# Rounding two weight blocks in turns, and the last block product of one group placed behind the first of the next

## The chip, the core and the metric

The kernel runs on one core of one Trainium2 chip. The metric is the time on the device in microseconds (us). The kernel before takes 807.48 us, the median of three runs that lie between 807.12 and 807.95 us. The execution that was profiled spans 805.8 us.

## The reference

The computation is a linear attention with a normalised output, followed by an MLP-Mixer block that mixes first over tokens and then over channels. All tensors are float32 outside; the four MLP weights come as float64.

```python
# q, k, v: 8 batches x 8 heads x 576 tokens x 64
kv  = einsum('bhsd,bhse->bhde', k, v)
o   = einsum('bhsd,bhde->bhse', q, kv)
o   = o / sqrt(mean(o * o, axis=-1) + 1e-06) * g_norm
x   = o.transpose(0, 2, 1, 3).reshape(8, 576, 512)
# token mixing: w_tok1 576 x 256, w_tok2 256 x 576
h   = maximum(x^T @ w_tok1, 0) @ w_tok2
u   = x + h^T
# channel mixing: w_ch1 512 x 1536, w_ch2 1536 x 512
out = u + maximum(u @ w_ch1, 0) @ w_ch2
```

## The kernel before

The kernel has three stages. In the first (to about 200 us) it loads queries, keys and values, runs attention for pairs of batches and token mixing for the pair before, and in between makes float32 weights out of the raw float64 words ("rounding"). In the second (200 to 273 us) it runs the channel mixing of a first group of tokens with a fast matrix product of seven block products in place of eight. In the third it runs the eight other groups with two levels of that scheme.

**Rounding.** A block of weights goes through one fetch (a DMA by the Sync engine's queue), one scaling on ScalarE, and six steps on VectorE. Each of the last five needs the one before; `power` begins a second tile, `part`. There are four buffers for raw blocks, and one for `part`.

```python
def decode(dst, raw):
    def scale():  nc.scalar.activation(dst, hi word of raw, AF.Copy, scale=2.0 ** -112)
    def clamp():  nc.vector.tensor_scalar(out=dst, in0=dst, ... min, max)
    def shift():  nc.vector.tensor_scalar(out=bits, in0=bits, 3, logical_shift_left)
    def sign():   nc.vector.scalar_tensor_tensor(out=bits, in0=hi word of raw, ..., in1=bits)
    def power():  nc.vector.tensor_scalar(out=part, in0=bits, 0xFF800000, bitwise_and)
    def lower():  nc.vector.scalar_tensor_tensor(out=part, in0=low word of raw, ..., in1=part)
    def both():   tensor_add(dst, dst, part)
    return scale, clamp, shift, sign, power, lower, both

def block(n, loads, dst):           # (fetch, scale, clamp, shift, sign, power, lower, both)
    def fetch():
        raw.append(stage.tile([P, n, 2], U32, name="raw", tag="raw", bufs=4))
        for o, i in loads(raw[0]):
            dma(o, i)
    ...
    return (fetch,) + decode(dst, turn)
```

Five token blocks (`w0` to `w4` in the lists below, the digit behind being the step) and fourteen channel blocks are rounded. The channel blocks run as one stream of 85 steps. A number in a list takes so many steps from it. `stream` of before rounds one block after the other; the scaling of the next block goes with `lower`, and the fetch of the block four further on with `both`:

```python
def stream(blocks, ahead=4):
    steps = [blocks[0][1]]
    for n, block in enumerate(blocks):
        steps += block[2:]
        for at, m, k in ((-2, n + 1, 1), (-1, n + ahead, 0)):
            if m < len(blocks):
                steps[at] = do(lambda *fs: [f() for f in fs], steps[at], blocks[m][k])
    return iter(steps)
```

**The order of the first stage.** Every engine takes its instructions in the order of these lists. `kv` and `a` are attention's products on TensorE, `e` their copies (ScalarE), `g` the gain (VectorE), `q` squares (ScalarE), `t` sums of squares, `m r i` mean, root and inverse, `s` eight scalings of a row (ScalarE), `l` and `lq` loads. `h` and `hr` are the first token product (`hr` ends with four ReLUs on ScalarE), `u` the second, and `z` the seed of a `u`, a copy by ScalarE into the PSUM bank (`ps_u`) to which the product then adds.

```python
def steady(n0, n1):
    return [
        "kv00 l00 e00 1 -s40", "h00 3", "kv01 l01 e01 1", "h01 3", f"a0 q00 g01 q01 g00 {n0}",
        "h10 1 t00 t01 2", "h11 4", "hr 2 z2", "a1 q10 g11 q11 g10 1", "kv10 l10 e10 t10 t11 m0 r0 1",
        "u0 i0 1", "kv11 l11 e11", "u1 1 s00", "u2 z4 1", "a2 q20 g21 q21 g20", "u3 s01 t20 t21",
        "u4 z6 1", "a4 q40 g41 q41 g40 lq0", "u5 s10 t40 t41 1", "a3 q30 g31 q31 g30 lq1",
        "u6 s11 t30 t31 m2 r2 1 i2 p20 p21 s30", f"u7 1 s31 {n1}", "u8 2"]
...
# start, middle (12 steps of the stream), steady(3, 1), steady(0, 0), last
```

**The first group's second product.** Seven block products, each of 24 matmuls, into four PSUM tiles; three of the tiles are used twice.

```python
def channel2_once(g):
    ...
    p1, p6, p7, p5 = (m_psum(shape, f"ps_w{n}") for n in (1, 6, 7, 5))
    ...
    def fourth():
        product(4, p7, False, True)
        tensor_add(quarter(1, 0), p7, quarter(1, 0))
        store(g, xg, 1)
    def third():
        product(3, p5, False, True)
        tensor_add(quarter(0, 1), p5, quarter(0, 1))
        store(g, xg, 0)
    return [first, sixth, second, seventh, fifth, fourth, third]
```

**The other groups.** PSUM has a pool `m` of six banks and a pool `c` of two. In each of the inner products the first small product goes into bank `a`; ScalarE (or VectorE) copies what is there into bank `c`, and TensorE then adds the second product to that copy, with `start=False`. The products are numbered places; what else is to be done goes `beside` a place.

```python
PLACE = {1: 0, 2: 8, 6: 3, 5: 4, 7: 6, 4: 9, 3: 12}      # the next inner product begins at 7
    def read_first():
        banks["c"] = late["c"].tile([P, DM], F32, name="ps_c")[:, :size]
        read(fit(banks["c"]), 0, 0)
    at(1, "a", True, False, read_first)
    at(6, "a", False, False, lambda: read(temp("u2", 2), 0, 1))
    ...
    at(2, "c", False, True, lambda: take(0, 0, "c", act))
```

**The seam between the two.** `weave` spreads sums of weights and their stores (32 of them) between the steps of the first group. Then come two "marking products": one matmul of 384 columns each into the two `c` banks, whose result nobody reads, so that TensorE has written the banks before copies are put there and added to.

```python
body = [step for pair in zip(channel2_once_steps, extra) for step in pair]
weave(body, lasts + [f for fs, _ in inner2 for f in fs] + [f for _, f in inner1])
fetch_x(1, 0)
fetch_x(1, 1)
for place in range(2):
    t = late["c"].tile([P, DM], F32, name="ps_c")
    step = do(matmul, t[:, :FQ], lhsT=w_ch1[:, 0, 0, :P], rhs=w_ch1[:, 0, 0], start=True, stop=True)
    put(place, step) if place else step()
```

Of the kernel before, what the change touches and what calls it, by code (L numbers as in the profile page):

```python
# [11 lines left out]
F32 = mybir.dt.float32  # L12
# [7 lines left out]
def kernel(  # L20
# [33 lines left out]
    P = 128  # L54
    B, S, DM = k.shape
# [11 lines left out]
    FQ = FH // 2  # L67
# [31 lines left out]
    w_ch1 = consts.tile([P, 4, 4, FQ], F32, name="w_ch1")  # L99
# [6 lines left out]
    def do(f, *a, **kw):  # L106
        return lambda: f(*a, **kw)

    late = {}
# [4 lines left out]
    def dma(o, i, engine=nc.sync):  # L114
        keep(engine.dma_start(o, i))  # L115

    def tensor_add(o, a, b, op=ALU.add, engine=nc.vector):
        keep(engine.tensor_tensor(out=o, in0=a, in1=b, op=op))  # L118
# [4 lines left out]
    def copy(o, a):  # L123
        keep(nc.scalar.copy(o, a))  # L124

    def matmul(*a, **kw):
        keep(nc.tensor.matmul(*a, **kw))  # L127
# [170 lines left out]
    def w2_of(n):  # L298
        i = {1: 0, 7: 1, 2: 2, 3: 3}
        return w_ch2[:, i[n]] if n in i else late["d2"][:, {5: 0, 6: 1, 4: 2}[n]]  # L300
# [263 lines left out]
    def fetch_x(g, i):  # L564

        if g < NG:
            if i == 0:
                xg[g] = late["xg"].tile([P, J, DM], F32, name="xg")
            dma(xg[g][:, ts(i, 2)], u_dram[g].rearrange("(t p) e -> p t e", p=P)[:, ts(i, 2)])
# [11 lines left out]
    blocks, blocks_dram = {}, {}  # L581
# [37 lines left out]
    def m_psum(shape, name):  # L619
        return late["m"].tile(shape, F32, name=name, tag="m")  # L620
# [17 lines left out]
    def r_tile():  # L638
        return late["r"].tile([P, 2, DH], F32, name="r", tag="r")
# [63 lines left out]
    def channel2_once(g):  # L703

        shape = [P, 2, DH]
        x = xg[g]
        quarter = lambda i, j: x[:, 2 * i:2 * i + 2, ts(j, DH)]

        def product(n, ps, start, stop):
            for p in range(2):  # L710
                for s in range(NS):
                    matmul(ps[:, p], lhsT=late["once"][n - 1][:, s, p], rhs=w2_of(n)[:, s],
                           start=(start and p == 0 and s == 0), stop=stop,
                           skip_group_check=True)

        p1, p6, p7, p5 = (m_psum(shape, f"ps_w{n}") for n in (1, 6, 7, 5))
        t1, u2, u3 = (r_tile() for _ in range(3))

        def first():
            product(1, p1, True, False)  # L720
            copy(t1, p1)

        def sixth():
            product(6, p6, True, True)
            tensor_add(u2, p6, t1)

        def seventh():
            product(7, p7, True, False)
            tensor_add(u3, p7, u2)
            tensor_add(quarter(0, 1), quarter(0, 1), u2)  # L730
            tensor_add(quarter(1, 0), quarter(1, 0), u2)

        def fifth():
            product(5, p5, True, False)
            tensor_add(u3, p5, u3)
            tensor_add(quarter(1, 1), quarter(1, 1), u3)

        def second():
            product(2, p1, False, True)
            tensor_add(quarter(0, 0), p1, quarter(0, 0))  # L740
# [12 lines that stand above are left out]
# [7 lines left out]
    def put(place, *steps):  # L760
        beside[place] += steps

    def outer(place, size, mul, to, base=None, act=copy, onto=False):

        banks, t = {}, {}

        def product(n, name, start, stop):
            if start:
                banks[name] = m_psum([P, size], f"ps_{name}")
            mul(n, banks[name], start, stop)

        def temp(n, bufs):
            t[n] = late["tmp"].tile([P, FQ], F32, name=n, tag=n, bufs=bufs)[:, :size]
            t[n] = fit(t[n])
            return t[n]

        def fit(flat):
            return flat if size == P else flat.rearrange("p (w t) -> p w t", w=W)

        def read(o, i, j):

            if base:
                tensor_add(o, fit(banks["a"]), base(i, j))
            else:
                copy(o, fit(banks["a"]))

        def read_first():
            banks["c"] = late["c"].tile([P, DM], F32, name="ps_c")[:, :size]
            read(fit(banks["c"]), 0, 0)

        def write(i, j, name, n):
            tensor_add(to(i, j), fit(banks[name]), to(i, j) if onto else t[n])

        def put_on(i, j, n):
            if onto:
                tensor_add(to(i, j), to(i, j), t[n])  # L800

        def take(i, j, name, act):
            if onto:
                tensor_add(to(i, j), banks[name], to(i, j))
            else:
                act(to(i, j), fit(banks[name]))

        def at(n, name, start, stop, *steps):
            def all_of():
                product(n, name, start, stop)  # L810
                for step in steps:
                    step()

            products[place + PLACE[n]] = all_of

        at(1, "a", True, False, read_first)
        at(6, "a", False, False, lambda: read(temp("u2", 2), 0, 1))
        at(5, "b", True, False)
        at(7, "a", False, False, lambda: read(temp("u3", 1), 1, 1))
        at(2, "c", False, True, lambda: take(0, 0, "c", act))  # L820
        put(place + PLACE[7] + (1 if onto else 2), do(put_on, 1, 1, "u3"), do(write, 1, 1, "b", "u3"))
        at(4, "a", False, True, lambda: take(1, 0, "a", copy) if onto else read(to(1, 0), 1, 0))
        put(place + PLACE[4], do(put_on, 0, 1, "u2"))
        at(3, "b", False, True)
        put(place + PLACE[3] + 1, do(write, 0, 1, "b", "u2"))
# [200 lines left out]
    def store(g, x, i):  # L1026
        x = x[g]
        if g < B:
            dma(out[g, ds(2 * i * P, 2 * P)].rearrange("(t p) e -> p t e", p=P),
                              x[:, 2 * i:2 * i + 2])  # L1030
        else:
            store_rest({B: x}, 2 * i)
            store_rest({B: x}, 2 * i + 1)
# [5 lines left out]
    def weave(body, fill):  # L1039
        done = 0  # L1040
        for n, step in enumerate(body):
            step()
            upto = len(fill) * (n + 1) // len(body)
            while done < upto:
                fill[done]()
                done += 1

    def stream(blocks, ahead=4):


        steps = [blocks[0][1]]
        for n, block in enumerate(blocks):
            steps += block[2:]
            for at, m, k in ((-2, n + 1, 1), (-1, n + ahead, 0)):
                if m < len(blocks):
                    steps[at] = do(lambda *fs: [f() for f in fs], steps[at], blocks[m][k])
        return iter(steps)

    def play(lines, after={}, **stages):
# [38 lines left out]
    for block in tok1[2:] + tok2:  # L1098
# [5 lines left out]


    start = [
        "kv00 e00 l00 j14 w01 w11 w02 w03 w04 w05 w06 w07 w12 w13 w14 w15 w16 w17", "kv01 j10 e01 l01 f0",
        "a00 g00 q00", "a01 g01 q01 t00", "a10 g10 q10 t01 m0 r0", "a11 g11 q11 t10 i0 p00 p01",
        "kv10 j6 t11 m1 r1 e10 i1 s10 p11", "kv11 j2 e11", "h000 h001 h002 h003", "a20 g20 q20", "a21 g21 q21 t20",
        "h010 t21 m2 r2", "a30 g30 q30 i2 p20", "a31 g31 q31 t30", "h011 t31 m3 r3 p21", "a40 i3 p30 g40 q40 p31",  # L1110
        "h012 h013 t40 m4 r4 w21 i4 s40 lq0 l10 l11"]
    middle = [
        "kv00 e00 w31 w22 w23 w24", "h10 w25 w26 w27 f1 -lq1 l00 w32 w33 w34", "kv01 e01 l01 w41 w35 w36 w37",
        "h11 f2 w42 w43 w44", "hr w45 w46 w47 f3", "a0 q00 g01 q01 g00 t00 t01", "u0 z2 1", "u1 1",
        "a1 q10 g11 q11 g10 t10 t11 m0 r0", "u2 i0 1", "kv10 e10 z4 s00", "u3 1 s01", "kv11 e11 1",
        "u4 1 z6", "a2 q20 g21 q21 g20 s10", "u5 t20 t21 2", "a4 q40 g41 q41 g40 lq0 l10 l11", "u6 t40 t41 2",
        "a3 q30 g31 q31 g30 lq1 s11", "u7 t30 t31 m2 r2 1 i2 p20 p21 s30", "u8 1 s31"]
# [38 lines left out]
    first = ExitStack()  # L1156
# [47 lines left out]
    n = len(sums1) // 3  # L1204
# [8 lines left out]
             lambda: [f() for f in outer_u(1)], lambda: [f() for f in inner_u(1, 0, 7)]]  # L1213
    extra += [lambda: None] * (len(channel2_once_steps := channel2_once(0)) - len(extra))
    body = [step for pair in zip(channel2_once_steps, extra) for step in pair]
    weave(body, lasts + [f for fs, _ in inner2 for f in fs] + [f for _, f in inner1])
    fetch_x(1, 0)
    fetch_x(1, 1)


    for place in range(2):
        t = late["c"].tile([P, DM], F32, name="ps_c")
        step = do(matmul, t[:, :FQ], lhsT=w_ch1[:, 0, 0, :P], rhs=w_ch1[:, 0, 0], start=True, stop=True)
        put(place, step) if place else step()
    for n, (_, f) in enumerate(inner2):
        put(8 + n, f)
    for g in range(1, NG):
# [42 lines left out]
```

## Time and profile before

| engine | busy us | share of 805.8 us | instructions |
|---|---|---|---|
| TensorE, matmuls | 788.6 | 98% | 7012 |
| TensorE, weight loads | 694.4 | 86% | 7012 |
| VectorE | 683.3 | 85% | 1308 |
| ScalarE | 302.2 | 38% | 838 |
| GpSimd | 79.6 | 10% | 75 |

The page calls the engines PE (matmuls), PEld (weight loads), DVE (VectorE), ACT (ScalarE), POOL (GpSimd) and SP (the Sync engine, whose queue issues the DMAs). A group of instructions is named by its line in the kernel, its engine, and output<-inputs. L163 is the scaling of a raw block, L166 to L187 are the rounding steps, L118 is every addition and subtraction, L121 a ReLU, L124 a copy, L421 the gain, L425 a square, L475 a row scaling, L127 every matmul. `raw<-in_moe_w_ch_dram` is the fetch of a raw channel block, `ps_w` the first group's second product, `ps_a`, `ps_b` and `ps_c` the inner products of the other groups.

Some rows of the groups that the change touches:

| what | count | mean ns of one |
|---|---|---|
| scaling of a channel block, 768 / 1024 columns (ScalarE) | 8 / 6 | 912 / 1160 |
| clamp, 768 / 1024 (VectorE) | 8 / 6 | 550 / 684 |
| shift, 768 / 1024 | 8 / 6 | 548 / 690 |
| sign, 768 / 1024 | 8 / 6 | 956 / 1329 |
| power, 768 / 1024 | 8 / 6 | 638 / 725 |
| lower, 768 / 1024 | 8 / 6 | 1116 / 1224 |
| both, 768 / 1024 | 8 / 6 | 1046 / 1216 |
| `ps_w` matmul, 256 columns (TensorE) | 168 | 379 |

Busy time is an average over stages that have different limits, and a busy TensorE includes matmuls whose ends are modelled. What a step is worth is therefore read from the wait that ends last in its own stretch of time. Idle time of an engine that nobody waits for costs nothing.

### The profile page before, as it was taken

The page shows a single profiled execution, that of the slowest core. Times are in us where ns is not written, and L with a number is a line of the kernel's source. Part 1 is how long each engine was busy: PE and PEld are TensorE (multiplying, and loading weights), DVE is VectorE, ACT ScalarE, POOL GpSimd, SP SyncE. Part 2 cuts the span into 40 slices and gives each one's busy share as a digit, 9 for nine tenths or more (in the row PEclk, how much of TensorE's full clock was granted, in tenths as well). Part 3 has the DMA queues.
Part 4 walks back from the last instruction along what each step waited for, and adds up shares of the span by engine and source line. Part 5 has one row for each costly group of instructions (what it writes and reads, how often), then busy time and mean ns, then how long its engine had stood idle before and what let it go on. Part 6 is the DMA issues. An engine that isn't in the chain of part 4 may idle for free.

```text
span 805.8 us, 17651 instructions
## 1 busy us (share of the span) xinstructions
PE 788.6 (98%) x7012; PEld 694.4 (86%) x7012; DVE 683.3 (85%) x1308; ACT 302.2 (38%) x838; POOL 79.6 (10%) x75
## 2 busy tenths in 40 slices
PE   6999999999999999999999999999999999999997
PEld 6645554544888899999999999999999999999997
DVE  4688989999886978978987997997898899799687
ACT  1357585664110134234234234332424423423331
POOL 1210101010000011012003003001101200300300
PEclk9999999999999999999999999999999999999999
DMA  9999998436458567468467648738836855863642
GB/s 289 320 345 351 334 354 304 158 119 208 150 175 294 194 210 239 131 221 267 149 201 240 201 153 259 234 118 262 265 119 217 262 166 181 250 201 123 218 147 83
DMA packets 97346, 175.51 MB, mean 218 GB/s; under 512 B 7024, under 2 KB 54128, under 8 KB 97264
## 3 DMA queue, kind: packets, MB, share of 16 engines
q1 hardware_dynamic: 95584, 172.65, 66.6%
q10 hardware_dynamic: 1680, 1.74, 0.7%
q8 instruction: 55, 0.90, 0.5%
q14 instruction: 27, 0.22, 0.1%
HBM read 137.79 MB, written 36.57 MB: 216 GB/s over the span
## 4 chain that ended last, share of the span: by engine, by line
PE 83%; DVE 6%; DMA 5%; ACT 3%; SPq 1%; issue 1%; ACTq 0%; DVEq 0%
PE ps_a L127 37%; PE ps_b L127 19%; PE ps_c L127 9%; PE ps_v L127 5%; PE ps_w L127 4%; PE ps_u L127 4%; DMA v_in<-in_v_dram 3%; PE ps_h L127 2%; ACT x L475 1%; SPq L115 1%; DMA raw<-in_moe_w_ch_dram 1%; DMA k_in<-in_k_dram 1%; DVE ms L442 1%; DVE part L187 1%; DVE x L421 1%; PE ps_o L127 1%
## 5 line engine op out<-in xcount | busy, mean ns | idle before, releaser
L124 ACT COPY u<-ps_a 128x128 f32<-128x128 f32 (+1 forms) x160 | 56.1, 351 | 156.6 <-PE ps_a L127 156.6
L118 POOL TENSOR_TENSOR v<-v,v 128x384 f32<-128x384 f32 (+1 forms) x48 | 61.4, 1301 | 532.8 <-ACT v L124 492.8
L127 PE MATMUL ps_b<-uT,sums 128*128 128x128 f32 x672 | 86.2, 276 | 0.0
L127 PEld LDWEIGHTS ps_b<-uT,sums 128*128 128x128 f32 x672 | 80.7, 192 | 0.2
L118 DVE TENSOR_TENSOR v<-v,v 128x768 f32<-128x768 f32 (+1 forms) x86 | 79.5, 932 | 1.1
L127 PE MATMUL ps_a<-uT,w_ch 128*128 128x128 f32 x576 | 78.9, 275 | 0.0
L124 ACT COPY ps_c<-ps_a 128x128 f32<-128x128 f32 (+1 forms) x80 | 26.9, 336 | 129.5 <-PE ps_a L127 129.5
L118 DVE TENSOR_TENSOR v<-ps_b,u 128x384 f32<-128x384 f32 x112 | 61.5, 549 | 12.3 <-PE ps_b L127 10.6
L127 PEld LDWEIGHTS ps_a<-uT,w_ch 128*128 128x128 f32 x576 | 71.4, 192 | 0.4
L127 PE MATMUL ps_u<-h,w_tok 128*128 128x512 f32 (+1 forms) x160 | 68.0, 608 | 1.6 <-ACT h L121 0.6
L127 PE MATMUL ps_h<-x,w_tok 128*128 128x512 f32 (+1 forms) x160 | 65.9, 604 | 0.0
L118 DVE TENSOR_TENSOR uT<-uT 128x512 f32<-128x512 f32 (+4 forms) x103 | 63.1, 629 | 0.8
L127 PE MATMUL ps_a<-uT,w 128*128 128x128 f32 x432 | 60.0, 275 | 0.0
L127 PEld LDWEIGHTS ps_a<-uT,w 128*128 128x128 f32 x432 | 54.0, 192 | 0.0
L127 PEld LDWEIGHTS ps_h<-x,w_tok 128*128 128x128 f32 (+1 forms) x160 | 25.9, 189 | 31.1 <-issue 28.3
L127 PEld LDWEIGHTS ps_u<-h,w_tok 128*128 128x128 f32 (+1 forms) x160 | 24.5, 178 | 31.9 <-issue 24.9
L121 ACT ACTIVATE v<-v 128x384 f32<-128x384 f32 (+1 forms) x86 | 42.5, 528 | 23.0 <-DVE v L118 22.5
L118 DVE TENSOR_TENSOR sv<-v 128x384 f32<-128x384 f32 x80 | 43.4, 551 | 8.9 <-ACT v L121 8.9
L118 DVE TENSOR_TENSOR xg<-xg,r 128x512 f32<-128x512 f32 x74 | 50.0, 686 | 0.7
L475 ACT ACTIVATE x<-x,inv 128x64 f32<-128x64 f32 x184 | 46.0, 336 | 9.6 <-DVE inv L461 9.6
L127 PE MATMUL ps_a<-sums,sv 128*128 128x128 f32 x336 | 47.1, 276 | 0.0
L127 PE MATMUL ps_a<-uT,sums 128*128 128x128 f32 x336 | 46.8, 275 | 0.0
(134 smaller groups left out, 1576.5 us busy)
## 6 DMA issues: line engine op xcount, KB each, us to landing
sums<-sums SPq DMA_DIRECT2D x112, 576.0 KB, 4.4
qT<-in_q_dram SPq DMA_DIRECT2D x8, 1152.0 KB, 9.6
xt<-u_dram SPq DMA_DIRECT2D x36, 256.0 KB, 4.0
blocks<-y SPq DMA_DIRECT2D x72, 128.0 KB, 2.7
uT<-blocks SPq DMA_DIRECT2D x36, 256.0 KB, 4.9
xg<-u_dram SPq DMA_DIRECT2D x18, 512.0 KB, 5.1
k_in<-in_k_dram SPq DMA_DIRECT2D x16, 512.0 KB, 9.2
u_dram<-x SPq DMA_DIRECT2D x16, 512.0 KB, 4.9
```

Of the source, the lines that this page charges most:

```text
L115: keep(engine.dma_start(o, i))
L118: keep(engine.tensor_tensor(out=o, in0=a, in1=b, op=op))
L121: keep(nc.scalar.activation(o, a, AF.Relu))
L124: keep(nc.scalar.copy(o, a))
L127: keep(nc.tensor.matmul(*a, **kw))
L187: keep(nc.vector.scalar_tensor_tensor(out=part[0], in0=raw()[..., 0], scalar=2.0 ** -52, in1=part[0], op0=ALU.mult, op1=ALU.mult))
L421: keep(nc.vector.tensor_mul(x, bank[c, h], g_sb.to_broadcast([P, number(c), D])))
L442: keep(nc.vector.tensor_reduce(stats_of(c)[0][:, h], sq[c, h], axis=AX.X, op=ALU.add))
L475: keep(nc.scalar.activation(x[:, k, h], x[:, k, h], AF.Copy, scale=inv[:, k, h]))
```

## The change

It has four parts. The stream of channel blocks takes the first three steps of one block (clamp, shift, sign) in turns with the last three of the block before (power, lower, both), so that neighbours on VectorE don't need each other; the scaling of the next block now goes with `shift`, and the fetch of a further block with `lower`. The lists of the first stage do the same by hand for the token blocks. The first group's tiles `p7` and `p5` come from the pool `c`, so that their products are TensorE's writes into these two banks, and the marking products go. And the step `third` leaves the woven part, and runs behind the first product of the next group, where TensorE has otherwise to wait for ScalarE's copy.

```diff
-        p1, p6, p7, p5 = (m_psum(shape, f"ps_w{n}") for n in (1, 6, 7, 5))
+        p1, p6 = (m_psum(shape, f"ps_w{n}") for n in (1, 6))
+        p7, p5 = (late["c"].tile(shape, F32, name="ps_c", tag="c") for _ in range(2))
...
-            banks["c"] = late["c"].tile([P, DM], F32, name="ps_c")[:, :size]
+            banks["c"] = late["c"].tile([P, DM], F32, name="ps_c", tag="c")[:, :size]
...
     def stream(blocks, ahead=4):
+        def all_of(*fs):
+            return do(lambda: [f() for f in fs])
         steps = [blocks[0][1]]
-        for n, block in enumerate(blocks):
-            steps += block[2:]
-            for at, m, k in ((-2, n + 1, 1), (-1, n + ahead, 0)):
-                if m < len(blocks):
-                    steps[at] = do(lambda *fs: [f() for f in fs], steps[at], blocks[m][k])
+        second = [None] * 3
+        for n in range(len(blocks) + 1):
+            first = list(blocks[n][2:5]) if n < len(blocks) else [None] * 3
+            if n + 1 < len(blocks):
+                first[1] = all_of(first[1], blocks[n + 1][1])
+            if second[1] and n - 1 + ahead < len(blocks):
+                second[1] = all_of(second[1], blocks[n - 1 + ahead][0])
+            steps += [f for pair in zip(first, second) for f in pair if f]
+            second = list(blocks[n][5:8]) if n < len(blocks) else second
         return iter(steps)
...
     start = [
-        "kv00 e00 l00 j14 w01 w11 w02 w03 w04 w05 w06 w07 w12 w13 w14 w15 w16 w17", ...
+        "kv00 e00 l00 j14 w01 w11 w02 w03 w04 w12 w05 w13 w06 w14 w07 w15 w16 w17", ...
     middle = [
-        "kv00 e00 w31 w22 w23 w24", "h10 w25 w26 w27 f1 -lq1 l00 w32 w33 w34", "kv01 e01 l01 w41 w35 w36 w37",
-        "h11 f2 w42 w43 w44", "hr w45 w46 w47 f3", ...
+        "kv00 e00 w31 w22 w23 w24", "h10 w41 w25 w32 w26 w33 w27 w34 f1 -lq1 l00", "kv01 e01 l01 w35 w42 w36 w43",
+        "h11 w37 w44 f2", "hr w45 w46 w47 f3", ...
...
     body = [step for pair in zip(channel2_once_steps, extra) for step in pair]
+    behind = body.pop(-2)
     weave(body, lasts + [f for fs, _ in inner2 for f in fs] + [f for _, f in inner1])
-    fetch_x(1, 0)
-    fetch_x(1, 1)
-    for place in range(2):
-        t = late["c"].tile([P, DM], F32, name="ps_c")
-        step = do(matmul, t[:, :FQ], lhsT=w_ch1[:, 0, 0, :P], rhs=w_ch1[:, 0, 0], start=True, stop=True)
-        put(place, step) if place else step()
+    put(0, behind, do(fetch_x, 1, 0), do(fetch_x, 1, 1))
```

## The prediction

> **What bounds the kernel now.** I read the page's first three parts, then the chain of waits, then the busy time by stretch, and then the stretches in which TensorE is not full.
>
> ```profile
> PE 788.6 (98%) x7012; PEld 694.4 (86%) x7012; DVE 683.3 (85%) x1308; ACT 302.2 (38%) x838; POOL 79.6 (10%) x75
> ...
> PE 83%; DVE 6%; DMA 5%; ACT 3%; SPq 1%; issue 1%; ACTq 0%; DVEq 0%
> ```
>
> TensorE is busy for 788.6 of 805.8 us and is 83% of the chain. A change that takes time off VectorE can therefore win only where TensorE waits: 17.2 us in all. The busy time by stretch (TensorE first, its weight loads, then VectorE, then ScalarE) says where that is:
>
> ```profile
> 60.00:80.00 20.00, 18.64 (x305) 10.28 (x304) 16.98 (x34) 14.82 (x49) 0.00 (x0) 1.00 1.03 351
> 80.00:100.00 20.00, 20.00 (x220) 10.02 (x216) 19.34 (x28) 9.77 (x31) 2.79 (x2) 1.00 1.08 336
> 100.00:120.00 20.00, 19.16 (x277) 10.48 (x270) 17.49 (x34) 16.26 (x47) 0.00 (x0) 1.00 1.07 350
> 120.00:140.00 20.00, 20.00 (x186) 9.93 (x185) 18.96 (x28) 12.89 (x41) 2.39 (x2) 1.00 0.86 323
> 140.00:160.00 20.00, 19.65 (x275) 10.49 (x274) 19.13 (x30) 12.54 (x33) 0.00 (x0) 1.00 0.40 138
> ```
>
> From 80 to 160 us, where most channel weights are rounded, VectorE is over 87% busy, and yet TensorE idles only 0.84 + 0.35 = 1.2 us there (80.00 less the four sums). The transfers are full to 140 us (shares near 1). So I asked what ScalarE, which opens each block's rounding with a scaling, waits for. The chain of waits between 98 and 124 us (start, length, work):
>
> ```profile
> 90.85 9.13 DMA raw<-in_moe_w_ch_dram
> ...
> 100.00 0.94 ACT w_ch L163
> 100.95 1.95 ACT h L121 x4
> 102.89 0.49 ACT ps_u L124
> 103.38 0.53 ACT sq L425
> ...
> 109.34 1.76 ACT x L475 x7
> 111.11 0.47 ACT x L124
> 111.58 0.48 ACT ps_u L124
> ```
>
> The reader is to see that a raw weight block lands at 99.98, that its scaling starts at 100.00, and that everything ScalarE owes TensorE (four ReLUs, the seed copies into `ps_u`, the squares) follows in file. The table of waits gives this one as 7.7 us. The next block's transfer, asked of the raw tile in the window where it is issued:
>
> ```profile
> L115 SPq DMA_DIRECT2D raw<-in_moe_w_ch_dram x1: 520/520/520, 96.2 to 96.2; - x1
> ...
> DMA to landing us min/median/max: 9.7/9.7/9.7
> ```
>
> It lands at 96.2 + 9.7 = 105.9. I come back to that number.
>
> **What the Trainium skill says.** "VectorE: DVE Perf Modes", section "The DRAIN you can't avoid", says that the next operation doesn't start until the pipe has emptied, so that a chain can't be made cheaper by order. The timeline of VectorE differs: after a clamp of 128x768 that takes 0.55 us, the dependent shift starts 0.58 us on (84.81 to 85.39), but an independent operation only 0.47 us on (72.82 to 73.29). I go by the trace: a dependence costs 0.11 us. "PSUM — Partial Sum Buffer", "The four PSUM rules", says that writes of VectorE and ScalarE neither set nor clear the bits that decide whether a matmul adds or overwrites; only matmuls do. That is what the marking products are for. The trace can show their time, not the bits. "Perfetto Trace Analysis", "Optimization Strategy", says to find the gaps of the busiest engine and what releases it; I follow it above.
>
> **The change part by part.** *Rounding in turns.* The block's six VectorE steps are clamp, shift, sign, power, lower, both; five of them depend on the one before. Fourteen channel blocks make 70 such pairs, of which 42 stand directly together in the timeline now (other work lies between the rest): 42 x 0.11 = 4.6 us of VectorE. As TensorE waits 1.2 us in 80 to 160, nearly all of it is off the path. For the token weights (128x576 steps) I laid the new order out from 47.04, where the first scaling ends: it finishes at 54.5 where it finished at 54.6, because the second block's first clamp must still wait for that scaling and now holds up the block before it. Worth 0.1.
>
> *What moves with it.* Counting the steps of the two orders: the scaling of block m stood at step 6m and stands at 6m - 5; the fetch of block m moves from 6(m - 4) + 7 to 6(m - 4) + 8, which is the same place in the DMA queue. So a block is scaled five steps earlier after an unchanged transfer. By the lines of `steady`, block 5's scaling goes from step 30 to 25, both between the squares at 91 us and the ReLUs: it still waits for 99.98. Block 6's scaling goes from step 36 (behind `kv11`, at 106.81 now) to step 31, in `hr`, directly behind the ReLUs, which end at 102.89. Its data lands at 105.9. ScalarE then stands 3.0 us and scales for 0.9 us, to 106.85, before the seed copy `z2` and the squares, which began at 102.89 and 103.38 before: 4.0 us later.
>
> What of it reaches TensorE: `u2` waits for the seed until 107.35, where it began at about 107.05: 0.3. The gain that follows the first square goes from 103.93 to 107.95, the mean from 106.31 to about 110.0, the inverse's end from 109.06 to 112.7, the eight scalings and the next seed (2.0 + 0.5 + 0.5) to 115.7. `u4` began at 112.11 with this seed, having waited for it, so TensorE is 3.6 us late there. Block 7's scaling (0.9 us) moves from step 42, where nobody waited, to step 37, in `u2`, ahead of the next squares, in a stretch where ScalarE is busy without a break: about 0.9 more. Some 4.7 us in this stretch. In the next pair block 12's scaling (1.06 us) goes behind the seed `z6`, and a `both` (1.22) before the last gains is replaced by a shift (0.69): the 1.12 us that TensorE waits at 160.8 falls by about 0.6.
>
> *The end of the first group.* The chain there:
>
> ```profile
> 236.70 36.26 PE ps_w L127 x168
> 272.96 0.65 PE ps_c L127 x2
> 273.60 0.67 PE ps_a L127 x6
> 274.27 0.65 PE ps_c L127 x2
> 274.92 0.84 PE ps_a L127 x6
> ```
>
> The two `ps_c` rows are the marking products: 1.30 us on TensorE's own path, removed whole. The second one filled the time in which ScalarE copies `ps_a`; the block product of 24 matmuls (168 / 7, 36.26 / 7 = 5.2 us) now fills it, so the 0.84 falls to 0.67 as well: 1.47 us. Against this stands VectorE's backlog: the add that frees the fourth product's bank ran at 271.98, though the product ended at 267.6, and the weaving over 13 places instead of 14 puts one more sum (0.47) in front of it. The copy into that bank then ends near 273.65, just as TensorE comes to need it; the last block product's add comes behind all the sums, near 277.6, and its bank is wanted again at about 277.65: a wait of up to 0.5. Net gain 1.0 to 1.5; I take 1.3.
>
> The sum: 807.5 - 0.1 + 4.7 - 0.6 - 1.3 = 810.2 us.
>
> **Rivals.** *All gain:* block 6's data lands before 103, or ScalarE isn't held by it. Then about -1.3 - 0.6 - 0.6 (part of the waits in 60 to 120) remains: 805.0. For it: transfers of the same size also took 6.2 us (the one issued at 71.4). Against it: the landing is governed by a full queue ahead of it, whose order doesn't change. *VectorE is the real bound:* 4.6 us less work on an engine 97% busy between 80 and 100 would give up to 4 us: 803.5. Against it: TensorE's 20.00 of 20.00 there. *A knock-on:* as clamps wait for the blocked scalings, VectorE stands from about 97.5 to 100.95, and the raw buffers are freed 2 to 3 us later, so that the fetches behind them and the key and value loads in the same queue are late: 813. Against it: those loads are used 15 us later. *A worse end:* the new wait for banks after the first group is 2 us, not 0.5: 812.
>
> **Range and chances.** I give the mechanism of block 6 about 70%, with 809 to 812 behind it, the all-gain case 20% near 805, the rest to worse. Predicted 810.2, range 805.0 to 813.0. Both ends are within 1% of the time before; 2% is 16 us, nearly all the idle time TensorE has. Faster by over 2%: 0.01; within 2%: 0.97; slower by over 2%: 0.02.
>
> **What would show it.** Right: in the changed kernel's waits a second wait of ScalarE for a raw channel block, near 103 and about 3 us long; TensorE waiting for `ps_u` copies near 107 and 112; no `ps_c<-w_ch` rows near 273; dependent rounding steps replaced by pairs 0.08 us inside each other. Wrong: ScalarE's only wait for raw weights still the one before 100 us, and less TensorE idle time between 100 and 125. It would also be wrong if the group boundary showed TensorE idle by over 1 us.

## The result, and the profile after

The changed kernel takes 813.56 us, the median of four runs (812.25 to 813.89), beside 807.3 us for the kernel before in the same comparison: a ratio of 1.0074, 95% interval 1.0057 to 1.0091. It is 6.3 us slower, where 2.9 had been predicted. The execution that was profiled is the fastest of the four (812.25 us); it spans 810.5 us, 4.7 more than before.

The page after, engines' busy time and the chain that ended last:

```profile
PE 786.6 (97%) x7008; PEld 692.1 (85%) x7008; DVE 678.9 (84%) x1308; ACT 301.2 (37%) x838; POOL 79.2 (10%) x75
...
PE 81%; DVE 8%; DMA 5%; ACT 4%; issue 1%; SPq 1%; ACTq 0%; DVEq 0%
```

VectorE has 4.4 us less to do and TensorE 2.0 (the marking products among it), and yet the span is longer: TensorE's idle time grew from 17.2 to 23.9 us. The busy time by stretch says where (the columns are TensorE, its weight loads, VectorE, ScalarE):

```profile
60.00:80.00 20.00, 18.17 (x294) 9.88 (x294) 16.10 (x32) 15.32 (x50) 0.00 (x0) 1.00 0.91 311
80.00:100.00 20.00, 20.00 (x218) 10.07 (x216) 17.56 (x27) 9.19 (x31) 2.39 (x2) 1.00 1.08 347
100.00:120.00 20.00, 15.16 (x225) 8.22 (x218) 12.55 (x24) 11.77 (x31) 0.00 (x0) 1.00 0.99 314
120.00:140.00 20.00, 19.14 (x245) 9.84 (x244) 19.50 (x33) 16.13 (x55) 2.39 (x2) 1.00 0.89 310
140.00:160.00 20.00, 20.00 (x250) 10.72 (x247) 18.09 (x29) 8.81 (x19) 0.00 (x0) 1.00 0.46 165
```

Between 100 and 120 us TensorE, VectorE and ScalarE all do less than before (19.16, 17.49 and 16.26 then). Three engines that are idle at once wait for a fourth thing. The chain of waits through that stretch (start, length, work) names it:

```profile
97.17 9.34 DMA raw<-in_moe_w_ch_dram
106.50 0.02 issue
106.53 0.91 ACT w_ch L163
107.43 0.48 ACT ps_u L124
107.91 0.53 ACT sq L425
...
109.08 0.95 DVE w_ch L174
...
113.64 0.36 DVE inv L461
...
116.52 0.07 ACT ps_u L124
```

Block 6's transfer lands at 106.50; its scaling is in front of the seed copy and the squares, and these in front of mean, root, inverse and the next seed. On TensorE (the last column is the idle time before, and what ended it):

```profile
102.74 1.99 PE L127 MATMUL ps_u<-h,w_tok 128*128 128x512 f32 x4 [1.02 <-ACT h L121]
...
111.90 0.93 PE L127 MATMUL ps_o<-kvp,qT 64*64 64x64 f32 x48 [1.56 <-ACT kvp L124]
...
117.05 1.98 PE L127 MATMUL ps_u<-h,w_tok 128*128 128x512 f32 x4 [2.12 <-ACT ps_u L124]
...
122.55 1.16 PE L127 MATMUL ps_o<-kvp,qT 64*64 64x64 f32 x64 [0.86 <-ACT sq L425]
```

These are 5.6 us of waits; in the kernel before, only the first and the third exist:

```profile
101.97 1.98 PE L127 MATMUL ps_u<-h,w_tok 128*128 128x512 f32 x4 [0.57 <-ACT h L121]
...
112.11 1.98 PE L127 MATMUL ps_u<-h,w_tok 128*128 128x512 f32 x4 [0.21 <-ACT ps_u L124]
```

The place of TensorE's instructions against the kernel before sums the whole up: +0.3 us when the first pair of batches is done (79 us), +5.7 at 129 us and still +5.7 when the first stage ends (205.85 against 200.17), +4.7 at the first `ps_b` behind the seam (280.30 against 275.59), +4.7 at the end.

The end of the first group, in the chain of waits:

```profile
278.32 0.61 DVE xg L118
...
279.02 0.47 ACT ps_c L124
...
279.53 0.49 PE ps_a L127 x2
```

No marking product is left, and the last block product lies behind the first product of the next group. From the first `ps_w` to the first `ps_b` it is 38.09 us instead of 39.06: 0.97 less.

### The profile page after: what moved, and what is told of

Same layout as the page of the kernel before. It is cut to its first block, busy times and chain, and to the rows that moved or that the text cites. A ratio compares the mean times of both kernels' runs of the same rounds, so it can differ in the third digit from the quotient of the medians.

```text
span 810.5 us, 17648 instructions
## 1 busy us (share of the span) xinstructions
PE 786.6 (97%) x7008; PEld 692.1 (85%) x7008; DVE 678.9 (84%) x1308; ACT 301.2 (37%) x838; POOL 79.2 (10%) x75
## 3 DMA queue, kind: packets, MB, share of 16 engines
q10 hardware_dynamic: 1680, 1.74, 0.7%
## 4 chain that ended last, share of the span: by engine, by line
PE 81%; DVE 8%; DMA 5%; ACT 4%; issue 1%; SPq 1%; ACTq 0%; DVEq 0%
PE ps_a L127 37%; PE ps_b L127 19%; PE ps_c L127 10%; PE ps_v L127 4%; PE ps_h L127 4%; PE ps_u L127 4%; PE ps_w L127 2%; ACT x L475 2%; DVE ms L442 1%; DMA k_in<-in_k_dram 1%; DMA raw<-in_moe_w_tok_dram 1%; DMA v_in<-in_v_dram 1%; DMA raw<-in_moe_w_ch_dram 1%; DVE x L421 1%; PE ps_o L127 1%
```

## The experiments

The theory: a scaling that stands in ScalarE's file ahead of its data holds everything behind it, and that is the loss; the turns themselves and the seam cost nothing. The rivals: the turns (VectorE's order) are the loss; the seam is; late key and value loads are.

### The parts alone: seam, turns, and the scaling's place

`seam_only` is the changed kernel with the stream and the lists of before. `turns_only` is the kernel before with the new stream of channel blocks and nothing else. `scale_early` is the kernel before, in which VectorE still rounds one block after the other, and only the scaling goes five steps ahead:

```diff
-        steps = [blocks[0][1]]
+        steps = [do(lambda *fs: [f() for f in fs], blocks[0][1], blocks[1][1])]
...
-            for at, m, k in ((-2, n + 1, 1), (-1, n + ahead, 0)):
+            for at, m, k in ((-1, n + 2, 1), (-1, n + ahead, 0)):
```

`turns_late_scale` is the changed kernel, turns and seam and all, with the scaling of the next block three steps later:

```diff
-            if n + 1 < len(blocks):
-                first[1] = all_of(first[1], blocks[n + 1][1])
...
+            if n + 1 < len(blocks):
+                at = second if n else first
+                at[2] = all_of(at[2], blocks[n + 1][1])
```

> The kernel before with the change at the seam alone: tiles p7 and p5 from the pool c, no marking products, the last block product behind the next group's first; lists and stream of rounding steps as before. If the loss of 6.3 us comes from the rounding stream (my theory), this runs about 1.0 us faster than before (1.30 us of marking products less about 0.3 us of new waits), 806.3, and TensorE starts the first group's product at the same time as before (ps_v near 200). If the seam itself costs time (rival: new waits for the two banks), it is slower than before.

> The kernel before with the new stream of rounding steps alone (two blocks in turns, scaling five steps earlier); token lists and seam as before. Theory: it carries the whole loss and lacks the gain of the seam, so 6 to 7.5 us slower than before, with two waits of ScalarE for raw channel blocks, the second of about 3 us near 103 us. Rival (the loss comes from the token lists or the seam): within 1 us of before.

> The kernel before with one thing moved: the scaling of block m goes with the last step of block m - 2 (step 6m - 5, as in the changed kernel) and VectorE's order stays one block after the other. Theory (ScalarE held by the transfer of block 6): the loss comes from the place of the scaling, so 4.5 to 7.5 us slower than before, with the second wait of ScalarE near 103 us. Rival (the order on VectorE, which puts longer steps before gains and sums, costs the time): within 1 us of before.

> The changed kernel with one thing moved: the scaling of the next block goes with the step both, three steps later, just before its own clamp (step 6m - 2). Block 6 is then scaled behind the roots in kv10, after about 106.5 us, when its data has landed. Theory: the second wait of ScalarE goes, and the kernel takes 805.5 to 807, about 1 us less than before (the seam), as the saved dependences on VectorE lie off TensorE's path. Rival 1 (order on VectorE costs the time): stays above 811. Rival 2 (VectorE is the bound once ScalarE is free): below 804.

| run | median us (runs) | before | ratio, 95% interval | first stage ends |
|---|---|---|---|---|
| seam_only | 807.02 (13) | 807.35 | 0.9993, 0.9985 to 1.0002 | 199.91 |
| turns_only | 813.88 (5) | 807.35 | 1.0077, 1.0063 to 1.0090 | 206.09 |
| scale_early | 813.51 (5) | 807.35 | 1.0067, 1.0055 to 1.0080 | 207.00 |
| turns_late_scale | 807.02 (21) | 807.35 | 0.9996, 0.9989 to 1.0002 | 199.33 |

("First stage ends" is the start of the first `ps_v` in the profiled execution; 200.17 for the kernel before.)

The loss follows the scaling's place, and nearly all of it is there without the new order of VectorE. With the old order and an early scaling it is there; with the new order and a later scaling it is gone. ScalarE's timeline in `scale_early` has the second wait for a raw block, with VectorE's order untouched:

```profile
100.44 2.05 ACT L121 ACTIVATE h<-ps_h 128x512 f32<-128x512 f32 x4
105.47 0.90 ACT L163 ACTIVATE w_ch<-raw 128x768 f32<-128x768 f32 x1 [2.98 <-DMA raw<-in_moe_w_ch_dram]
106.27 0.57 ACT L124 COPY ps_u<-x 128x512 f32<-128x512 f32 x1
```

and that of `turns_late_scale` has it no longer: the seed copy follows the ReLUs directly, and the scaling comes after its data, which landed at 107.17.

```profile
101.70 2.06 ACT L121 ACTIVATE h<-ps_h 128x512 f32<-128x512 f32 x4
103.60 0.64 ACT L124 COPY ps_u<-x 128x512 f32<-128x512 f32 x1
...
107.93 0.91 ACT L163 ACTIVATE w_ch<-raw 128x768 f32<-128x768 f32 x1
```

`scale_early` doesn't lose its time in quite the same places, though. At 129 us it is 4.7 us behind the kernel before, and the changed kernel 5.7: about 1 us, or somewhat more, comes with the turns. After that, `scale_early` loses some time to the clock. Behind a wait of 1.74 us, TensorE's granted clock is at half for 3.4 us (the third number from the end), and 16 matmuls of a second token product take 7.26 us, 1.7 more than the 5.57 in the changed kernel:

```profile
168.20:171.60 3.40, 3.40 (x7) 1.44 (x5) 3.37 (x8) 1.61 (x5) 0.00 (x0) 0.50 0.89 295
```

The same is seen once more there, from 117.0 to 120.4, and nowhere in the two profiles of the changed kernel but in the last 3 us. The only one of the five runs of `scale_early` with a mean clock of 1.0 took 812.19 us, 4.8 more than before. So the scaling's place alone is worth some 4.7 us, and not the full 6.2 of the medians.

So "the turns are the loss" and "the seam is the loss" fall. `turns_late_scale` came out at the upper edge of its expectation (807.02, of 805.5 to 807); `seam_only` fell short of its own (807.02, not 806.3). The seam alone changes the time by something between -1.2 and +0.2 us, by its interval.

### The same file, an earlier transfer

If the wait is for the transfer, then the changed kernel must recover without any change to ScalarE's order, when the raw block lands earlier. In the one queue, four key and value loads stand directly in front of the fetch of block 6, and four others in front of that of block 5. `fetch_first` moves the first four behind the fetch, `fetch_both` all eight. `after_again` is the changed kernel once more.

```diff
 fetch_first
-            ... "kv01 l01 e01 1", "h01 3", f"a0 ...
+            ... "kv01 e01 1", "h01 3 l01", f"a0 ...
 fetch_both, in addition
-            "kv00 l00 e00 1 -s40", "h00 3", ...
+            "kv00 e00 1 -s40", "h00 3 l00", ...
```

> The changed kernel with one thing moved: in the steady list the load l01 of keys and values stands behind the three steps after it, so that the fetch of block 6 is issued before it, some 5 us earlier (near 92 us instead of 97.2), and should land near 102 instead of 106.5. VectorE's and ScalarE's orders stay as changed. Theory (what costs is that ScalarE reaches block 6's scaling before its transfer has landed): the second wait of ScalarE (2.9 us) goes, and 3.5 to 5 us of the loss with it: 808.5 to 810. The 0.9 us for block 7's scaling ahead of the squares stays. Rival (the scaling's mere place among ScalarE's work costs the time, landed or not): stays above 812.

> As fetch_first, and the load l00 also stands behind the fetch of block 5, which should land near 95.5 instead of 100.8. Theory: ScalarE no longer waits for raw channel blocks at all, the ReLUs follow their product at once, and TensorE's wait for them (1.0 us) goes too: about 0.5 to 1 us below fetch_first. Rival (the transfers are bound by the full DMA engines, not by their place in the queue): blocks 5 and 6 land as late as before, no gain.

> The changed kernel once more, for a second profile, as the first one (812.25) was the fastest of four runs by 1.1 us. If the extra time is the landing of blocks 5 and 6, which varies, the second profile shows TensorE's first product of the first group at 206 to 207 us (205.9 in the first profile). If it is in the third stage: a longer time from there to the end (599.6 us in the first profile).

| run | median us (runs) | before | ratio, 95% interval | first stage ends |
|---|---|---|---|---|
| fetch_first | 810.29 (5) | 807.59 | 1.0035, 1.0022 to 1.0048 | 203.14 |
| fetch_both | 809.75 (9) | 807.59 | 1.0029, 1.0020 to 1.0039 | 201.63 |
| after_again | 813.69 (6) | 807.59 | 1.0072, 1.0060 to 1.0084 | 206.56 |

`fetch_first` takes 3.4 us off the changed kernel, just under the expected 3.5 to 5, with one instruction group moved in a queue and none on an engine. Block 6's fetch is issued at 93.24 instead of 97.17 and lands at 103.08, before ScalarE comes to it:

```profile
101.86 2.04 ACT L121 ACTIVATE h<-ps_h 128x512 f32<-128x512 f32 x4
103.77 0.93 ACT L163 ACTIVATE w_ch<-raw 128x768 f32<-128x768 f32 x1
104.57 0.62 ACT L124 COPY ps_u<-x 128x512 f32<-128x512 f32 x1
```

At the end of the first stage 3.0 us of loss are left (203.14 against 200.17). Most of that is the scaling itself in front of the chain: TensorE still waits 1.41 us for a `ps_u` copy at 114.32 and 0.88 us for squares at 119.84, where `turns_late_scale` has 0.61 and 0.18. The rest is 0.4 us from the first pair and the wait for the ReLUs behind block 5 (1.13 us, 0.57 in the kernel before). `fetch_both` brings block 5 from 101 to 96.4, and the wait for the ReLUs (1.02 us in the changed kernel) goes:

```profile
96.44 0.93 ACT L163 ACTIVATE w_ch<-raw 128x768 f32<-128x768 f32 x1 [4.71 <-DMA raw<-in_moe_w_ch_dram]
...
102.31 0.92 ACT L163 ACTIVATE w_ch<-raw 128x768 f32<-128x768 f32 x1 [1.47 <-DMA raw<-in_moe_w_ch_dram]
```

Against the expectation, block 6 still lands at 102.28 and holds ScalarE for 1.47 us, and TensorE's waits of 1.32 us for `ps_u` and 0.85 for squares stay as in `fetch_first`. The gain of `fetch_both` over `fetch_first` is 1.5 us at the end of the first stage in the profiles and 0.5 in the medians, whose intervals overlap. The loads that were put off made nobody wait, against the rival of late loads.

In `after_again` both answers of the expectation hold. The first stage ends at 206.56, 0.7 later than in the first profile, and from there to the end it takes 606.7 us, 2.1 more than the first profile's 604.6 (810.47 - 205.85; the 599.6 above is a slip).

### Together, and loads alone

`best_mix` joins the later scalings and both moved loads, and keeps the weaving at 14 places, with an empty one where the last block product was. `loads_behind` is the kernel before with only the loads moved.

```diff
 best_mix: turns_late_scale and fetch_both, and
-    behind = body.pop(-2)
+    behind, body[-2] = body[-2], lambda: None
 loads_behind, on the kernel before
-            "kv00 l00 e00 1 -s40", "h00 3", "kv01 l01 e01 1", "h01 3", ...
+            "kv00 e00 1 l00 -s40", "h00 3", "kv01 e01 1", "h01 3 l01", ...
```

> The turns with the late scaling, both loads behind the fetches, and the seam with the last block product's place in the weaving kept empty (14 places again), so that no more sums stand before the add that frees the bank. Theory: TensorE loses its wait for the ReLUs (0.6 to 1.0 us), and 0.2 us at the seam: 805.3 to 806.5, 1 to 2 us below before. Rival (the loads, issued later, are then late for the next pair): above 807.

> The kernel before with the two loads of keys and values behind the fetches of blocks 5 and 6, and nothing else. Theory: block 5 lands near 95 us instead of 100, the ReLUs follow their product at once, TensorE's wait of 0.57 us at 101.4 goes and what hangs on it: 0.5 to 1.5 us faster than before. Rival: the wait only moves to the loads: same as before.

`best_mix` takes 805.38 us (7 runs; before 807.59): ratio 0.9970, interval 0.9959 to 0.9980. `loads_behind` takes 806.26 us (18 runs; before 807.45): 0.9986, 0.9979 to 0.9993. Both beat the kernel before; the loads alone are about half of it. TensorE's waits in `best_mix` (us in total, times, longest):

```profile
...
PE ps_o L127 <- ACT sq L425: 2.1, 2, 1.6
PE ps_a L127 <- ACT ps_c L124: 1.0, 1, 1.0
PE ps_o L127 <- ACT kvp L124: 0.6, 1, 0.6
```

There is no `ps_u<-ACT` left, neither for ReLUs nor for seeds. The 1.0 us for a copy into `ps_c` is the seam: with 14 places the backlog of VectorE's sums moves to another bank, and the wait with it (at 276.10).

### Where the seam's gain goes

The profile had 0.97 us less at the seam, and the time of the seam alone hardly any. In the repeated changed kernel TensorE waits 0.98 us at 295.21 for a fetch of weight sums that had been issued right behind the two 512 KB fetches of `xg`. `seam_x_later` is `seam_only` with these two at place 20 instead of place 0. `best2` is `best_mix` with the same, and with the sums of the inner products held back to just before their use; `best2_in_file` is `best2` with the stream and lists of before, so that the pair shows what the turns are worth together with the later scalings (two steps earlier than in the order of before).

```diff
-    put(0, behind, do(fetch_x, 1, 0), do(fetch_x, 1, 1))
+    put(0, behind)
+    put(20, do(fetch_x, 1, 0), do(fetch_x, 1, 1))
 best2, in addition
-    weave(body, lasts + ... + [f for _, f in inner1])
+    weave(body, lasts + ... + [f for _, f in inner1[:2]])
+    for n in range(2, 7):
+        put(7 * n - 4, inner1[n][1])
```

> seam_only with the two fetches of the next group's tile xg moved from place 0 to place 20. In the second profile of the changed kernel TensorE waited 1.0 us at 294 us for a fetch of sums that stood in the DMA queue behind these fetches, and they behind the store of the last block product. Theory: with them out of the way the seam keeps its gain: 806.0 to 806.6 where seam_only took 807.0, and no wait of TensorE for sums. Rival (the seam's gain is lost elsewhere, at the late wait for u near 696 us): 807.0 as before.

> best_mix with the seam freed of its two new waits: five of the sums in place go behind the last block product's add, to the places where they are needed (VectorE's backlog made TensorE wait 0.95 us at 275 us for the bank of that product), and the fetches of xg to place 20. Theory: 0.9 us less at the seam, 804.0 to 804.8. Rival (the time comes back in the third stage, where the sums now crowd VectorE): 805.4.

> best2 with the rounding steps one block after the other again (stream and lists of before, its scaling at step 6m), the loads behind the fetches. It tells what the turns on VectorE are worth once ScalarE isn't held. If the 4.4 us of VectorE's busy time lie off TensorE's path, as I predicted: the same as best2 within 0.5 us. If they matter: 1 to 3 us slower than best2.

| run | median us (runs) | ratio to before (807.45), 95% interval |
|---|---|---|
| seam_x_later | 807.95 (13) | 1.0005, 0.9997 to 1.0013 |
| best2 | 806.67 (13) | 0.9994, 0.9986 to 1.0002 |
| best2_in_file | 808.14 (13) | 1.0004, 0.9996 to 1.0012 |

My expectation fell: place 20 stands in front of another fetch of sums, and that one now landed 7.6 us after its issue instead of 5.4 in `seam_only`. TensorE's timeline in `seam_x_later`:

```profile
293.66 0.91 PE L127 MATMUL ps_a<-uT,sums 128*128 128x128 f32 x6 [1.72 <-DMA sums<-sums]
```

`best2` missed its range (804.0 to 804.8) too: its first inner product waits 1.02 us for a sum of weights at 273.25, as I read it because the weaving is thinner with the sums held back. Between `best2` and `best2_in_file` the profile has 1.3 us at the end of the first stage (197.43 against 198.74); the medians differ by 1.5, in the range of "they matter", but there is a wait of 2.3 us for sums in the profile of the second and of 1.2 in that of the first, so that I rely on the first stage only. These are single profiles, and two of the changed kernel differ by 0.7 us there (205.85 and 206.56); but the two waits that the kernel before has near 156 and 162 us (0.26 and 1.12) are absent in `best2` and there in `best2_in_file` (0.29 and 1.12).

The last two runs put the two fetches behind a fetch of sums each, on the seam alone and on `best_mix`:

```diff
-    put(0, behind, do(fetch_x, 1, 0), do(fetch_x, 1, 1))
+    put(0, behind)
+    put(22, do(fetch_x, 1, 0))
+    put(36, do(fetch_x, 1, 1))
```

> The seam change alone, with its two 512 KB fetches of xg apart and each behind a fetch of weight sums (places 22 and 36) instead of together at place 0. If those two fetches in front of a fetch of sums are where the seam's 1 us goes: no wait of TensorE for sums over 0.5 us, the seam alone then gains 0.7 to 1.2 us over before (806.2 to 806.8 at a before of 807.4). If the gain is lost in scatter elsewhere (a late transfer of another kind later in the run): 806.9 to 807.6, as the seam alone measured, with a wait of another name in its place.

> best_mix (turns, scalings three steps later, both loads behind the fetches of raw blocks, seam with 14 places) with the same two fetches at places 22 and 36. If the fetches are the loss: 804.4 to 805.2, no wait for sums. If not: 805.3 to 806.0, as best_mix.

`seam_x_behind` takes 806.70 us (13 runs; before 807.45), ratio 0.9990, interval 0.9982 to 0.9998; the products that waited start without a wait (one of 0.35 us for sums is left at 696.51):

```profile
291.78 0.83 PE L127 MATMUL ps_a<-uT,sums 128*128 128x128 f32 x6
```

`best3` takes 805.32 us (8 runs): 0.9972, 0.9961 to 0.9984, no different from `best_mix`, whose wait of 0.95 us for `ps_c` it still has (at 275.80). The first is in the range of "the fetches are the loss", the second in that of "not". What is shown: two fetches in front of a fetch of sums can make TensorE wait 1.7 us, and put behind it they don't. That they are what the seam alone lost is not: its interval overlaps that of `seam_only`, whose profile had another wait instead (0.58 us at 696.64, for an addition).

## Why the prediction was wrong

The mechanism was the predicted one, and its signs are there: a second wait of ScalarE for a raw channel block of 2.87 us (3.0 predicted), a wait of TensorE for `ps_u` (2.12 us, at 117.05 where 112 was written), pairs of rounding steps 0.08 us inside each other, no `ps_c<-w_ch` near 273. What failed is the sum of what reaches TensorE: four of its terms were too small or too favourable. The first pair lost 0.3 where 0.1 was to be gained, the stretch behind block 6 lost 5.3 and not 4.7, the next pair gained nothing and not 0.6, and the seam gained 1.0 and not 1.3. That is 1.9 of the 3.4 us between 810.2 and 813.56. Where the other 1.5 comes from stays open.

**VectorE: the total right, partly by luck.** 4.6 us less were predicted for the channel blocks, and 683.3 - 678.9 = 4.4 were measured in all. But `turns_only`, where the channel stream alone is new, is at 679.9: the channel blocks make 3.4. Most of the rest is the token blocks (17.50 us busy from 40 to 60 us before, 16.85 after), for which the prediction counted no VectorE time. Little of it reached the path in the changed kernel. The timeline of VectorE shows independent neighbours 0.47 us apart, where a dependent clamp and shift had 0.58:

```profile
87.03 0.55 DVE L166 TENSOR_SCALAR w_ch<-w_ch 128x768 f32<-128x768 f32 x1
87.50 0.55 DVE L183 TENSOR_SCALAR part<-w_ch 128x768 uint32<-128x768 uint32 x1
87.97 0.55 DVE L170 TENSOR_SCALAR w_ch<-w_ch 128x768 uint32<-128x768 uint32 x1
```

The section of the Trainium skill that the prediction names, "The DRAIN you can't avoid" in "VectorE: DVE Perf Modes", has the next operation wait until the pipe has emptied, and adds that one which is not held starts earlier. This trace agrees (0.47 us after the start of a step of 0.55), so page and timeline don't differ there. What a dependence costs, 0.11 us after a clamp, is the trace's own number.

**"Some 4.7 us in this stretch": 5.3 measured** (+0.3 at 79 us to +5.7 at 129). The step that failed is `u4`, "3.6 us late": it is 117.05 - 112.11 = 4.9 us late, as the seed ended at 117.0 and not at 115.7. Of these 1.3 us, 0.6 is the landing: I took it as unchanged at 105.9, but this fetch was issued 1.0 us later (97.17 against 96.19) and landed at 106.50. That delay comes with the turns and not with the blocked scaling: the fetch goes out at 97.26 in `turns_late_scale` and at 95.94 in `scale_early`. The other 0.7 lies between the gain and the mean: 2.8 us (108.47 to 111.25), where the prediction has 2.05 (107.95 to 110.0) and the kernel before 2.4. The step of VectorE that now stands between the gain and the sums of squares is a sign (0.95) in place of a shift (0.47). (The 4.7 isn't quite the sum of its own terms: the lateness at `u4` contains that at `u2`, so 3.6 + 0.9 = 4.5.) Two waits I hadn't counted: the ReLUs behind block 5, which landed 0.8 us later (TensorE's wait grew from 0.57 to 1.02), and the second copy of `kvp`, behind the root in ScalarE's file (1.56 us at 111.90). The latter adds nothing of its own, as I read it: without it TensorE would have waited that much longer for the seed. Block 7's scaling, 0.9 predicted, is the 0.86 before the squares at 122.55: right.

**"Worth 0.1" in the first pair: it lost 0.3** (a `kvp` copy 0.26 us late at 67.60, squares 1.57 instead of 1.33). The token weights themselves end at 54.52, as predicted; the loss comes behind them. These waits are in `turns_late_scale` as well (0.54 and 1.57), so they are not block 6's, and in `turns_only` (0.26 and 1.57), so they are not the token lists' either. `scale_early` has the second alone (1.57), so the wait for `kvp` comes with the turns of the channel stream. What makes the second was not taken apart.

**"The 1.12 us at 160.8 falls by about 0.6": it fell by 0.04.** VectorE was quicker, and block 12's scaling took its place in front of the squares on ScalarE. I had counted the replaced `both` and not the 1.11 us of that scaling as ahead of squares:

```profile
165.72 1.11 ACT L163 ACTIVATE w_ch<-raw 128x1024 f32<-128x1024 f32 x1
166.74 0.64 ACT L425 ACTIVATE sq<-ps_r 128x256 f32<-128x256 f32 x2
```

`scale_early`, with the early scaling and VectorE's old order, waits 1.74 us for these squares. So the turns did take 0.66 off this wait (1.74 to 1.08), about what was predicted, and the scaling's place had added 0.62 (1.12 to 1.74). With the scalings later the gain is there: TensorE has no wait of 0.2 us or more from 130 to 200 us in `turns_late_scale`, where the kernel before has 0.26 and 1.12.

**"Net gain 1.0 to 1.5; I take 1.3" at the seam: 0.97 in the profile,** and 0.3 (interval -0.2 to 1.2) in the time of the seam alone. The marking products did go. The add that frees the fourth product's bank ended at 278.94, behind VectorE's sums, and TensorE waited 0.23 us for the copy behind it; 0.16 more is lost by 284.65, behind the copy into the other bank, which follows the last block product's add (to 283.28).

**What the sum lacked** is the third stage. In the fastest run: 0.3 + 5.3 + 0.0 - 1.0 = 4.6, as the profile has it. That makes 807.5 + 4.6 = 812.1 us, and the median is some 1.5 us above it. The profile of the repeat (815.05 us) is 6.4 us late when the first stage ends, 5.4 behind the seam, and then loses another 2.1, of which 0.98 is the fetch of sums at 295.21. The rest is waits too small to name, and it stays open how much of the 1.5 in the median is due to each. The clock doesn't tell the runs apart: of the ten runs of the changed kernel, five have a mean clock of 0.997 or 0.998 and a median of 813.76 us, and five have 0.999 or 1.0 and 813.36.

**The rivals.** "All gain" was wrong since the landing came after 103; `fetch_first`, where it lands at 103.08, doesn't reach that either, as the scaling itself stays in front of the chain. "VectorE is the real bound" fell with `scale_early` and `turns_late_scale`. The time came out near the 813 of "a knock-on", but by chance. Raw fetches behind the blocked scaling did go out 3.9 us later (104.18 against 100.25), yet the first key load behind them landed at 112.84 against 112.65, and TensorE waited for none of these loads. "A worse end" didn't come: 0.23 and 0.16 us.

## What to carry to other kernels

Look at what an instruction stands in front of before moving it forward in an engine's list: an in-order engine that reaches an instruction too early is held by it, and everything behind it is, here 2.9 us of waiting that became, with the scalings' own time in front of squares and seeds, 5 us on the path. Move a step that depends on a transfer no earlier than the transfer lands in the trace, and when a change of order lightens one engine, check the order of the others that came along with it. If a transfer is what the path waits for, first look at its neighbours in the queue: moving loads that nobody was waiting for behind it gained 1.2 us on the old kernel without a change to any engine's work.

## What was not expected of the hardware

- A fetch of weight sums (576 KB) takes 3.7 us when it stands alone, and 7.6 us behind two fetches of 512 KB issued 1.0 and 0.6 us ahead of it (and one of 256 KB, 1.4 us ahead), both in `seam_x_later`. In the changed kernel the fetch of a raw channel block (128x768) took 4.5 us when issued at 73.71, and 9.3 when issued at 97.17 behind four key and value loads. A landing can't be told from the size alone.
- The same VectorE work in another order is 4.4 us shorter, and this was worth nothing in the medians as long as ScalarE held the path (`turns_only` 813.88, `scale_early` 813.51). With the scalings late and the loads moved, the first stage was 1.3 us shorter with the turns and the later scalings than without, in one profile of each.
- TensorE's granted clock went to 0.50 for 3.4 us at a time: twice in the profile of `scale_early` (from 117.0 and 168.2) and once in that of `turns_only` (from 113.2). The second cost `scale_early` about 1.7 us. The one in `turns_only` cost next to nothing, as it filled a wait: TensorE's wait for the seed there is 0.43 us in place of 2.12.
